# w_out times phi for four row tiles at once in the column groups, whole output rows stored for the last twelve token tiles, and another step list

## The chip, the cores and the metric

One core of one Trainium2 chip runs the kernel. The number that counts is the device time of one execution in microseconds, the median of several runs. The engines are named as in the profile: PE (matrix products; PEld is its weight loading), DVE, ACT and POOL (element-wise work), SP (whose queue issues all DMAs of this kernel).

## The reference

Three stages follow one another. The first is a linear attention with a decaying state, for 4 batches, 8 heads, 768 tokens and head size 48:

```python
for t in range(S):
    cur = einsum('bhd,bhe->bhde', u * k[t], v[t])
    y[t] = einsum('bhd,bhde->bhe', r[t], state + cur)
    state = w[t][..., None] * state + einsum('bhd,bhe->bhde', k[t], v[t])
```

Its output, as 3072 tokens by 384, goes through `h = x @ w_in` (384 to 2048), `g = h * cos(h)` and `x2 = g @ w_out` (2048 to 384). The third stage is a soft mixture: `logits = x2 @ phi` (32 slots), a softmax over the tokens gives the 32 slot inputs, eight experts of two matrices each (`w1`: 384 to 1024, relu, `w2`: 1024 to 384) work on 4 slots each, and a softmax over the slots mixes the slot outputs into 3072 rows of 384. `w_in` and `w_out` come as float64, everything else as float32.

## The kernel before

The kernel never forms `x2`. As only `x2 @ phi` and sums over tokens are needed, it computes `P = w_out @ phi` (2048 by 32) once and takes the logits as `g @ P`; the slot inputs come from sums of `g` over tokens, multiplied by `w_out` at the end.

Work is cut into small named steps, and the string `HEAD` (from line 899) gives their order, about 1980 of them. Each step issues the instructions of one function on one or two engines, and every engine, and SP's queue, works through its own instructions in the order of the list. `name.j` is a step on attention tile j (24 tiles of 128 tokens), `name.g.i` one on token group g (12 groups of 256 tokens) and block i (8 blocks of 256 columns of the hidden layer).

- Weights. `raw` loads a piece of `w_in` ("i") or `w_out` ("o"), and `abs` (ACT), `mx`, `d1`, `d2a`, `d2b` (DVE) turn its float64 bits into float32; the last one of `w_out` is `d2b.o.7`. `whi`, `wn`, `wc` split `w_in` into two halves. `raw` has two buffers.
- `P`. For each of the 16 row tiles m of `w_out`, `oT` (line 416) transposes the tile with three products, `oc` (line 421) copies it to SBUF on ACT, and `om` (line 427) multiplies it with `phi`: three float32 products with a stationary operand of 128 by 128 and 32 moving columns. `ps` (line 430) copies four tiles of `P` to SBUF.
- Attention. `wT`, `kT`, `rT` transpose inputs on PE, `scan`, `sr`, `sp`, `ks`, `L`, `mask`, `bo`, `z`, `st` are DVE's, `A`, `U`, `kN`, `y`, `yb` are PE's, `ru`, `bv`, `zl` POOL's.
- Hidden layer. `h` (lines 451 to 453) is nine products for 128 columns; `turns` (ACT), `rest` (DVE), `cos` (ACT), `mul` (DVE) make `g`; `gT` transposes it (PE), `gc` copies it (ACT), `l` (line 496) adds the block to the logits with four products in the column groups: stationary operands of 32 columns whose outputs lie in the four quarters of the partitions.
- Softmax over tokens: `sum`, `lc`, `max`, `exp`, `xt`, `xr`, `xd`, `dT`, `dc`, `ltok`, `E`, `es`. The last group uses ACT's Exp itself (line 540), the others go by Silu. The step `tab` (line 688) runs one small Exp on ACT.
- `att` closes the attention's buffers and queues the first six expert matrices; `we.6` to `we.10` load others into buffers that the hidden layer has given up.

Behind the list, `hidden(e)` uses `w1[e]`, `expert_out(i, e)` (line 826) uses `w2[e]` for columns 0 to 255 (i = 0) or 256 to 383 (i = 1), with four products at a time in the column groups, and `outputs(i, n0)` (line 843) multiplies the mixing weights with the slot outputs, copies the result to SBUF and stores it. The first four token tiles use the float32 copies `cf` and `so`; the others use `cr` and `sr`, three rounded parts stacked in 96 rows. All of columns 0 to 255 are stored as pairs of token tiles, in runs of 1024 bytes, and then all of columns 256 to 383 as fours, in runs of 512 bytes.

Of the kernel before, what the change touches and what calls it, by code (L numbers as in the profile page):

```python
# [21 lines left out]
def rwkv_moe_kernel(ctx: ExitStack, tc: tile.TileContext, r, k, v, w, u, w_in, w_out, phi, w1, w2, cst, out):  # L22
# [612 lines left out]
    if True:  # L635
# [112 lines left out]
        with tc.manual_schedule(engines=ORDERED):  # L748
# [94 lines left out]
            def outputs(i, n0, tile_=None):  # L843

                cols = parts[i]
                n = cols.stop - cols.start
                nt = 512 // n
                t0, t1 = (0, nt) if tile_ is None else (tile_, tile_ + 1)
                ps = pb(f"o{i}_{n0}_{t0}").rearrange("p (t f) -> p t f", t=nt)[:, 0:t1 - t0]
                if n0 % 6 == 0 and t0 == 0:  # L850
                    obs[i] = wu_p.tile([128, 6, nt, n], F32, tag=f"wu{n0 // 6 if i == 0 else 2}", name=f"ob{i}_{n0}")
                ob = obs[i][:, n0 % 6, t0:t1]
                for t in range(t0, t1):
                    tt = n0 * nt + t
                    if tt < 4:

                        nc.tensor.matmul(ps[:, t - t0], lhsT=cf[:, tt * 128:(tt + 1) * 128], rhs=so[:, cols], start=True, stop=True)
                    else:
                        nc.tensor.matmul(ps[:, t - t0], lhsT=cr[:, tt // NB, tt % NB, :], rhs=sr[:, cols], start=True, stop=True)
                if tile_ is not None and n0:  # L860
                    nc.vector.tensor_copy(ob, ps)
                    if t1 < nt:
                        return
                    ob, t0 = obs[i][:, n0 % 6], 0
                else:
                    (nc.vector.tensor_copy if n0 % 2 else nc.scalar.copy)(ob, ps)
                nc.sync.dma_start(out[(n0 * nt + t0) * 128:(n0 * nt + t1) * 128, cols].rearrange("(t p) f -> p t f", p=128), ob)
# [35 lines left out]
A.0 z.0.1 mask.0 wn.0.0 raw.o.0 st.0.1 lk.2 kT.1 rz.0.1 rz.0.0 lv.1 mx.o.3 d1.o.3 ks.1 d2a.o.3 wn.0.1 wc.0.1 d2b.o.3 lw.2 y.0 lz.2
abs.o.0 lr.2 lw.3 z.1.0 lv.2 A.1 yb.0 mx.o.0 d1.o.0 abs.o.2 mx.o.2 wc.0.0 kN.1 ksn.1 d2a.o.0 d2b.o.0 oT.1 xh.0 xl.0 d1.o.2 raw.i.1
abs.o.1 mx.o.1 d1.o.1 oT.0 oc.0 oc.1 om.0 d2a.o.1 d2a.o.2 wT.2 wf.2 d2b.o.1 om.1 lz.1 raw.i.4 mask.1 d2b.o.2 oT.3 oT.2 oc.2 oc.3
U.1 ru.1 bo.1 oT.4 rz.1.0 abs.i.1 st.1.0 z.1.1 rz.1.1 st.1.1 bv.1 scan.2 kT.2 abs.i.4 om.2 ks.2 y.1 yb.1 om.3 mx.i.4 xh.1 xl.1
mx.i.1 d1.i.1 d2a.i.1 kN.2 d2b.i.1 h.0.2.0 h.0.2.1 ksn.2 oc.4 rT.2 sr.2 sp.2 L.2 raw.i.3 lr.3 lw.4 d1.i.4 z.2.0 d2a.i.4 d2b.i.4
whi.1 wn.1.0 h.0.0.0 wc.1.0 h.0.0.1 turns.0.0 rz.2.0 oT.5 wT.3 oc.5 rest.0.0 ru.2 bo.2 bv.2 U.2 wf.3 A.2 cos.0.0 wn.1.1 st.2.0
turns.0.2 wc.1.1 mul.0.0 gT.0.0 om.4 lk.3 kT.3 mask.2 z.2.1 st.2.1 scan.3 ks.3 rest.0.2 whi.4 abs.i.3 mx.i.3 d1.i.3 sr.3 d2a.i.3
d2b.i.3 sp.3 wn.4.0 kN.3 ksn.3 wn.4.1 h.0.1.0 h.0.1.1 wc.4.0 lw.5 raw.i.6 abs.i.6 lv.4 whi.3 gc.0.0 lk.4 mx.i.6 cos.0.2 wc.4.1  # L910
wn.3.0 oT.7 wc.3.0 rT.3 wn.3.1 raw.i.5 d1.i.6 rz.2.1 oc.7 y.2 wc.3.1 d2a.i.6 turns.0.1 abs.i.5 mul.0.2 L.3 A.3 wT.4 h.0.3.0
d2b.i.6 wf.4 mx.i.5 d1.i.5 z.3.0 whi.6 mask.3 wn.6.1 ps.0 wc.6.1 rest.0.1 scan.4 yb.2 om.5 cos.0.1 xh.2 kT.4 d2a.i.5 ru.3 lk.5
wn.6.0 mul.0.1 sr.4 lv.3 ks.4 l.0.1 xl.2 sp.4 d2b.i.5 U.3 st.3.0 raw.i.7 abs.i.7 z.3.1 mx.i.7 oT.6 wc.6.0 gT.0.2 gc.0.2 lr.5 bo.3
st.3.1 d1.i.7 oc.6 d2a.i.7 h.0.3.1 gT.0.1 wT.5 wf.5 kN.4 h.0.4.0 gc.0.1 d2b.i.7 lz.3 whi.7 wn.7.0 whi.5 h.0.4.1 wn.5.1 lr.4
# [144 lines left out]
```

## Time and profile before

| | |
|---|---|
| median of 3 runs | 563.93 us (563.49 to 565.99) |
| the profiled execution | 567.16 us |
| its span, first to last instruction | 565.4 us |
| PE, PEld, DVE busy | 516.0, 447.6, 438.7 us |
| ACT, POOL busy | 313.3, 123.2 us |
| moved by DMA | 61.75 MB read, 4.72 MB written |

The profiled execution is one run; its time is its span and 1.8 us around it. Busy time of PE contains the latency of its pipeline, so an engine that is 97% busy may still wait a little between products. The span has four parts: the filling up to about 123 us, in which the weights are decoded and the first attention tiles and hidden blocks start; a long stretch up to 520.5 us, where the list of steps ends; the wait for the last expert matrices up to 544.1 us; and the output up to 565.4 us.

### The profile page before, as it was taken

The numbers are of one execution on the slowest core, as the hardware profiler recorded it, in microseconds if no ns is written. First come the engines' busy times: TensorE is split into PE (matmuls) and PEld (weight loads), VectorE is DVE, ScalarE is ACT, GpSimd is POOL, SyncE is SP. The second block draws the span as 40 slices with busy tenths as digits, with TensorE's granted clock in tenths as the row PEclk, the third lists the DMA queues.
The fourth block names the chain that finished last, engine by engine and source line by source line (L and its number), as shares of the span: only waits on it lengthen the run. The fifth ranks groups of instructions, "written<-read, shape, count | busy, mean of one in ns | idle before, by whom it ended". The sixth has DMA issues, their size and how long they took to land.

```text
span 565.4 us, 16220 instructions
## 1 busy us (share of the span) xinstructions
PE 516.0 (91%) x6846; PEld 447.6 (79%) x6846; DVE 438.7 (78%) x823; ACT 313.3 (55%) x657; POOL 123.2 (22%) x163
## 2 busy tenths in 40 slices
...
GB/s 206 297 167 88 144 179 126 128 71 16 112 55 75 68 33 58 44 72 43 45 86 39 61 16 90 41 106 51 59 59 12 6 225 378 180 237 225 405 202 275
DMA packets 146712, 67.52 MB, mean 119 GB/s; under 512 B 127568, under 2 KB 134736, under 8 KB 146640
## 3 DMA queue, kind: packets, MB, share of 16 engines
...
q8 instruction: 54, 0.88, 0.7%
...
HBM read 61.75 MB, written 4.72 MB: 118 GB/s over the span
## 4 chain that ended last, share of the span: by engine, by line
PE 58%; DVE 27%; ACT 6%; DMA 4%; issue 3%; SPq 0%; DVEq 0%; ACTq 0%
PE h L451 9%; PE h L453 8%; PE h L452 8%; PE gT L483 5%; PE l L496 3%; PE y L288 3%; PE E L592 3%; DVE g L475 3%; DMA we<-in_moe_w_dram 3%; PE A L208 3%; DVE L L222 3%; DVE g L467 3%; DVE L L187 2%; PE U L259 2%; DVE qt L156 2%
## 5 line engine op out<-in xcount | busy, mean ns | idle before, releaser
L451 PE MATMUL h<-x,wu 128*128 128x256 f32 x573 | 168.8, 295 | 3.9 <-DVE g L475 3.6
L453 PE MATMUL h<-x,wu 128*128 128x256 f32 x573 | 162.3, 283 | 0.0
L452 PE MATMUL h<-x,wu 128*128 128x256 f32 x573 | 162.3, 283 | 0.0
L451 PEld LDWEIGHTS h<-x,wu 128*128 128x128 f32 x573 | 110.3, 193 | 6.1 <-DVE g L475 5.2
L452 PEld LDWEIGHTS h<-x,wu 128*128 128x128 f32 x573 | 110.4, 193 | 0.2
L453 PEld LDWEIGHTS h<-x,wu 128*128 128x128 f32 x573 | 110.0, 192 | 0.0
L471 ACT ACTIVATE g<-g,half_pi 128x512 f32<-128x512 f32 (+1 forms) x97 | 69.2, 718 | 44.0 <-DVE g L467 43.4
L463 ACT ACTIVATE g<-h 128x512 int32<-128x512 f32 x96 | 56.9, 595 | 59.1 <-PE h L453 39.1
L467 DVE SCALAR_TENSOR_TENSOR g<-g,h 128x512 f32<-128x512 int32 x96 | 64.9, 678 | 27.5 <-ACT g L463 26.8
L475 DVE TENSOR_TENSOR g<-g,h 128x512 f32<-128x512 f32 x96 | 64.7, 678 | 22.9 <-ACT g L471 22.2
L251 POOL TENSOR_TENSOR bv<-vz,bo 64x384 f32<-64x384 f32 x48 | 41.9, 873 | 151.8 <-DVE bo L243 56.6
L488 ACT COPY gt<-gT 128x512 f32<-128x512 f32 x92 | 53.4, 584 | 28.5 <-PE gT L483 22.5
L483 PE MATMUL gT<-cs,g 128*128 128x128 f32 x384 | 58.9, 278 | 2.4 <-DVE g L475 1.7
L169 POOL TENSOR_TENSOR ru<-rn,u_b 128x384 f32<-128x384 f32 x24 | 27.7, 1156 | 123.2 <-DVE bo L243 46.0
L483 PEld LDWEIGHTS gT<-cs,g 128*128 128x128 f32 x384 | 43.6, 142 | 12.3 <-issue 6.5
L274 ACT COPY rzs<-z 64x192 f32<-64x192 f32 x96 | 33.4, 348 | 9.5 <-DVE z L269 8.4
L156 DVE TENSOR_TENSOR_SCAN qt<-wf,one_b 128x520 f32<-128x520 f32 x24 | 31.9, 1329 | 6.5 <-ACT wf L151 6.4
L187 DVE TENSOR_TENSOR L<-rT,pt 64x512 f32<-64x512 f32 x48 | 32.9, 686 | 4.3 <-PE y L288 2.8
L222 DVE TENSOR_TENSOR L<-A,cs 64x512 f32<-64x512 f32 x48 | 33.1, 689 | 1.2
L193 POOL MEMSET L<- 64x512 f32 x32 | 16.6, 520 | 69.3 <-PE y L288 68.3
L496 PE MATMUL l<-g,p_sb 128*32 128x256 f32 x384 | 29.8, 385 | 1.5 <-DVE g L475 1.5
L164 DVE TENSOR_TENSOR_SCAN pt<-wf,ini_f 128x520 f32<-128x520 f32 x24 | 30.2, 1258 | 0.2
...
## 6 DMA issues: line engine op xcount, KB each, us to landing
...
```

The lines of the kernel that those rows point to most:

```text
L187: nc.vector.tensor_tensor(out=L[h, a], in0=ps[h], in1=segs(pt, 0, C)[h], op=ALU.mult)
L222: nc.vector.tensor_tensor(out=L[h, a], in0=ps[h], in1=mask[h].unsqueeze(1).to_broadcast([64, NS, C]), op=ALU.mult)
L451: nc.tensor.matmul(hp, lhsT=wh, rhs=xh[:, c, :], start=(c == 0), stop=False)
L452: nc.tensor.matmul(hp, lhsT=wh, rhs=xl[:, c, :], start=False, stop=False)
L453: nc.tensor.matmul(hp, lhsT=wl, rhs=xh[:, c, :], start=False, stop=(c == KD - 1))
L463: nc.scalar.activation(gt.bitcast(I32), hp, AF.Copy, bias=0.25, scale=1.0 / TWO_PI)
L467: nc.vector.scalar_tensor_tensor(out=gt, in0=gt.bitcast(I32), scalar=-TWO_PI, in1=hp, op0=ALU.mult, op1=ALU.add)
L471: nc.scalar.activation(gt, gt, AF.Sin, bias=half_pi[:, 0:1])
L475: nc.vector.tensor_tensor(out=gt, in0=gt, in1=hp, op=ALU.mult)
L483: nc.tensor.transpose(ps[:, tt, mm, :], gt[:, mm, tt * 128:(tt + 1) * 128], ident)
L488: (nc.vector.tensor_copy if NBK * g + i >= ATT and i in (1, 2) else nc.scalar.copy)(t, pend.pop(("gT", g, i)))
L496: nc.tensor.matmul(lps_t[g][32 * mm:32 * mm + 32, 0:G], lhsT=p_sb[:, m, :], rhs=g_t[g, m // 2][:, m % 2, :], start=(m < 4), stop=(m >= MF ...
```

## The change

It has three parts.

First, `P`. The transposed tiles `wt` take their buffers from the twelve that `gc` uses. `om` now works on four row tiles at once: `phi` is the stationary operand (32 columns), the four transposed tiles are the moving operands of 128 columns, and the outputs lie in the four quarters of the partitions. This leaves the transpose of `P`, so `pc` copies it to SBUF (ACT), `pT` transposes it (one product on PE) and `ps` copies it into `p_sb`. The 16 `om` steps become four, and four `pc` and four `pT` are new.

Second, the output. Columns 0 to 255 of token tiles 0 to 11 are stored as before, in pairs; the last twelve token tiles wait for both halves of the slot outputs and are stored as whole rows, two rows to a partition, 3072 bytes in one run; columns 256 to 383 of the first twelve come last. Only tiles 0 and 1 use `cf`. The slot outputs are copied by ACT and DVE, half each, and the copies of the output alternate between ACT and DVE. `expert_out(1, e)` is spread otherwise between the stores.

Third, `HEAD` has the same steps apart from those of `P`, in another order. A function for `wlo` on another engine is added, and no step uses it.

```diff
     def e_oc(m):
-        wt_t[m] = aw.tile([128, KD, 128], F32, tag="wt", name=f"wt{m}")
+        wt_t[m] = gt_p.tile([128, KD, 128], F32, tag="gt", name=f"wt{m}")
         nc.scalar.copy(wt_t[m], pend.pop(("woT", m)))
-    def e_om(m):
-        if not pt_ps:
-            pt_ps[0] = ps_m.tile([128, MF, SL], F32, tag="m", name="pp")
+    def e_om(u_):
+        ps = ps_m.tile([128, 512], F32, tag="m", name=f"pt{u_}")
         for c in range(KD):
-            nc.tensor.matmul(pt_ps[0][:, m, :], lhsT=wt_t[m][:, c, :], rhs=phi_sb[:, c, :], start=(c == 0), stop=(c == KD - 1))
+            for q in range(4):
+                nc.tensor.matmul(ps[32 * q:32 * q + 32, 0:128], lhsT=phi_sb[:, c, :], rhs=wt_t[4 * u_ + q][:, c, :], start=(c == 0), stop=(c == KD - 1))
+        pt_ps[u_] = ps
+    def e_pc(u_):
+        wt_t["p", u_] = aw.tile([128, 128], F32, tag="pts", name=f"pts{u_}", bufs=1)
+        nc.scalar.copy(wt_t["p", u_], pt_ps[u_][:, 0:128])
+    def e_pT(u_):
+        pend["P", u_] = tps(f"P{u_}")[:, 0:128]
+        nc.tensor.transpose(pend["P", u_], wt_t["p", u_], ident)
     def e_pw(u_):
-        nc.scalar.copy(p_sb[:, 4 * u_:4 * u_ + 4, :], pt_ps[0][:, 4 * u_:4 * u_ + 4, :])
+        nc.scalar.copy(p_sb[:, 4 * u_:4 * u_ + 4, :], pend.pop(("P", u_)).rearrange("p (q s) -> p q s", q=4))
...
+            def store(i, tag, tiles, n):
+                cols = slice(0, DM) if i is None else parts[i]
+                w = cols.stop - cols.start
...
+                        if tt < 2 and i == 0:
+                            nc.tensor.matmul(ps[:, t], lhsT=cf[:, tt * 128:(tt + 1) * 128], rhs=so[:, cols], start=True, stop=True)
+                        elif i is None:
+                            o = tiles[0] * 128 + b0 + t
+                            nc.tensor.matmul(ps[:, t], lhsT=crt[:, o:o + 255:2], rhs=sr[:, cols], start=True, stop=True)
...
+                    pend["ob"] = 1 - pend.get("ob", 0)
+                    (nc.scalar.copy if pend["ob"] else nc.vector.tensor_copy)(ob[:, b0:b0 + k], ps)
+                dst = out[t0:t0 + len(tiles) * 128, cols]
+                nc.sync.dma_start(dst.rearrange("(p t) f -> p t f" if i is None else "(t p) f -> p t f", p=128), ob)
...
-            nc.scalar.copy(so[:, parts[0]], ops[0][:, 0:256])
-            expert_out(1, 0)
-            outputs(0, 0, 0)
+            copy_so(0)
+            store(0, "wu0", [0], 0)
             slots_out(0)
+            store(0, "wu0", [1], 1)
             slots_round(0)
-            outputs(0, 0, 1)
-            outputs(0, 1, 0)
-            outputs(0, 1, 1)
-            for n0 in range(2, 5):
-                outputs(0, n0)
-            for e in range(1, 4):
+            for e in range(2):
                 expert_out(1, e)
-            for n0 in range(5, 9):
-                outputs(0, n0)
-            for e in range(4, NE):
+            for t in range(2, 8, 2):
+                store(0, "wu0", [t, t + 1], t)
+            for e in range(2, 5):
                 expert_out(1, e)
-            nc.vector.tensor_copy(so[:, parts[1]], ops[1][:, 0:128])
-            for n0 in range(9, 12):
-                outputs(0, n0)
+            for t in range(8, 12, 2):
+                store(0, "wu0", [t, t + 1], t)
+            for e in range(5, NE):
+                expert_out(1, e)
+            copy_so(1)
             slots_out(1)
             slots_round(1)
-            for n0 in range(6):
-                outputs(1, n0)
+            for t in range(12, 18, 2):
+                store(None, "wu1", [t, t + 1], t - 12)
+            for t in range(18, 24, 2):
+                store(None, "wu2", [t, t + 1], t - 18)
+            for t in range(0, 12, 4):
+                store(1, "wu3", [t, t + 1, t + 2, t + 3], t)
```

Of the list, three places are spoken of below. Where the weights' decoding ends:

```diff
-h.1.1.0 h.1.1.1 mask.5 tab turns.0.6 gc.0.5 rest.0.6 gT.0.4 kT.6 cos.0.6 oc.10 sr.6 sp.6 mul.0.6 ks.6 oT.13 oc.13 rz.5.0 om.10
-gc.0.4 ps.2 wf.7 rT.6 mx.o.7 d1.o.7 h.1.0.0 oT.12 oc.12 d2a.o.7 d2b.o.7 close l.0.5 om.13 oT.14 oT.15 om.12 turns.1.1 bv.4 ru.6
+oc.11 wT.6 lw.8 U.5 om.2 gc.0.4 rest.0.7 cos.0.7 wf.6 L.5 A.5 mx.o.7 d1.o.7 bo.4 bv.4 mul.0.6 oT.13 oc.13 mask.5 d2a.o.7 d2b.o.7
+close h.1.0.0 gT.0.6 oT.12 pc.2 pT.2 oc.12 lr.6 gc.0.6 scan.6 h.1.0.1 ru.6 mul.0.7 sr.6 ps.2 bo.6 oT.14 oT.15 oc.14 l.0.5 oc.15
+om.3 kT.6 turns.1.0 rest.1.0 rz.4.0 h.1.1.0 gT.0.7 ks.6 pc.3 pT.3 ps.3 z.5.0 st.5.0 z.5.1 st.5.1 cos.1.0 mul.1.0 y.4 l.0.7 rT.6
```

The new place of `tab` (before, it stood as shown above):

```diff
+turns.9.2 rT.23 dT.8 h.9.4.0 xl.22 cmb.1.5 zl.23 rest.9.2 sp.23 cos.9.2 gT.9.1 L.23 gc.9.1 h.9.4.1 gT.8.6 h.9.5.0 h.9.5.1 gc.8.6
+xh.21 xl.21 dc.8 tab turns.9.4 cmb.0.5 rest.9.4 turns.9.5 h.9.6.0 gT.9.3 h.9.6.1 rest.9.5 cos.9.5 mul.9.2 A.23 ltok.8 E.8.0 E.8.1
```

And the end, where the last hidden block was `h.11.7` in two halves and is now the undivided `h.11.4`:

```diff
-rest.11.4 gT.11.2 dT.10 ltok.10 gc.11.0 mul.11.5 cos.11.4 mul.11.4 h.11.7.0 dc.10 turns.11.7.0 h.11.7.1 turns.11.7.1 rest.11.7.0
-cos.11.7.0 rest.11.7.1 mul.11.7.0 l.11.5 cos.11.7.1 E.10.0 mul.11.7.1 l.11.7 gT.11.4 gc.11.2 gc.11.4 gT.11.5 sum.11 lc.11 max.11
+rest.11.5 cos.11.5 gT.11.2 gc.11.2 xd.10 h.11.4.0 h.11.4.1 turns.11.4 dT.10 mul.11.5 ltok.10 gT.11.6 dc.10 E.10.0 E.10.1 gc.11.3
+rest.11.4 cos.11.4 mul.11.4 l.11.5 mul.11.7.0 l.11.7 sum.11 we.6 we.10 gT.11.5 lc.11 gc.11.5 gT.11.4 gc.11.6 max.11 quart.11
```

## Rows read from the trace of the kernel before

**Rows 1.** The page: busy time of each engine.
```profile
PE 516.0 (91%) x6846; PEld 447.6 (79%) x6846; DVE 438.7 (78%) x823; ACT 313.3 (55%) x657; POOL 123.2 (22%) x163
```

**Rows 2.** Four stages: PE, PEld, DVE, ACT, POOL busy (count), clock, DMA share, GB/s.
```profile
20.00:123.00 103.00, 84.91 (x967) 70.95 (x965) 92.89 (x141) 56.81 (x109) 26.22 (x24) 0.90 0.63 148
123.00:520.50 397.50, 386.68 (x5263) 345.85 (x5263) 317.24 (x625) 236.18 (x506) 83.69 (x103) 1.00 0.37 88
520.50:544.10 23.60, 23.00 (x390) 13.83 (x390) 8.86 (x25) 8.05 (x21) 5.86 (x9) 1.00 0.88 335
544.10:565.40 21.30, 13.61 (x204) 11.65 (x204) 7.19 (x13) 6.13 (x13) 0.00 (x0) 0.90 0.73 224
```

**Rows 3.** DVE in order of time (start, duration): the last step of the decoding.
```profile
121.47 0.90 DVE L374 SCALAR_TENSOR_TENSOR wo_sb<-rawo,ao 128x768 int32<-128x768 int32 x1
```

**Rows 4.** Groups by line: w_out times phi (busy, mean ns, idle before).
```profile
L427 PE MATMUL pp<-phi_sb,wt 128*128 128x32 f32 x96 | 13.2, 280 | 0.6 <-ACT wt L421 0.6
```

**Rows 5.** PE in order of time (start, duration): `l`, `om`, two `oT`, `om`, `h`.
```profile
130.75 0.64 PE L496 MATMUL l<-g,p_sb 128*32 128x256 f32 x8
131.32 0.85 PE L427 MATMUL pp<-phi_sb,wt 128*128 128x32 f32 x6
132.01 0.85 PE L416 MATMUL woT<-cs,wo_sb 128*128 128x128 f32 x6
132.70 0.75 PE L427 MATMUL pp<-phi_sb,wt 128*128 128x32 f32 x6
133.29 0.36 PE L451 MATMUL h<-x,wu 128*128 128x256 f32 x1
```

**Rows 6.** The chain that ended last: start, time on it, what.
```profile
463.82 0.86 PE l L496 x16
469.91 0.87 PE gT L483 x8
...
500.27 0.12 PE h L452
...
528.61 15.46 DMA we<-in_moe_w_dram
...
546.80 1.29 PE o L857 x6
...
551.41 1.88 PE so L826 x64
```

**Rows 7.** PE in order of time: one `gT` step, then two `l` steps.
```profile
448.53 0.60 PE L483 MATMUL gT<-cs,g 128*128 128x128 f32 x4
449.06 1.07 PE L496 MATMUL l<-g,p_sb 128*32 128x256 f32 x16
```

**Rows 8.** DVE work of an attention tile: two pieces of the chain, one group by line.
```profile
347.32 0.69 DVE ks L199
409.60 1.15 DVE qt L156
...
L269 DVE TENSOR_TENSOR z<-st_state,qt 128x192 f32<-128x192 f32 x44 | 21.0, 478 | 0.8
```

**Rows 9.** `turns` for half a block (order of time) and for a whole one (group).
```profile
510.25 0.38 ACT L463 ACTIVATE g<-h_7b 128x256 int32<-128x256 f32 x1
...
L463 ACT ACTIVATE g<-h 128x512 int32<-128x512 f32 x96 | 56.9, 595 | 59.1 <-PE h L453 39.1 <-PE l L496 16.7 <-PE gT L483 2.9
```

**Rows 10.** DMA: 550-553 us (1024-byte stores), 559-562 (512-byte), 524-539 (loads), 562-566 in fortieths.
```profile
DMA packets 1058, 1.02 MB, mean 340 GB/s; under 512 B 63, under 2 KB 1058, under 8 KB 1058
...
DMA packets 1734, 0.86 MB, mean 288 GB/s; under 512 B 54, under 2 KB 1734, under 8 KB 1734
...
DMA packets 2022, 6.06 MB, mean 404 GB/s; under 512 B 62, under 2 KB 62, under 8 KB 2019
...
DMA  9999999999999999996100000000000000000000
```

**Rows 11.** ACT in order of time: one of its table loads.
```profile
123.41 1.28 ACT L471 ACT_TABLE_LOAD   x1
```

More of the change, by code (lines that the diff above doesn't have):

```diff
@@ L841, in rwkv_moe_kernel @@
             obs = {}
[L843 to L867, printed above, removed]
@@ L869, in rwkv_moe_kernel, with copy_so @@
+            def copy_so(i):
+                c, h = parts[i], (parts[i].start + parts[i].stop) // 2
+                nc.scalar.copy(so[:, c.start:h], ops[i][:, 0:h - c.start])
+                nc.vector.tensor_copy(so[:, h:c.stop], ops[i][:, h - c.start:c.stop - c.start])
             expert_out(0, 0)
@@ L903 @@
[L903 to L914, printed above, removed]
@@ L915 @@
-raw.o.5 bv.3 turns.0.3 rest.0.3 rz.3.0 scan.5 ksn.4 wn.5.0 turns.0.4 rest.0.4 wc.7.0 raw.o.4 lz.4 abs.o.4 mx.o.4 wc.5.0 wc.5.1
-rz.3.1 ru.5 bo.5 rT.4 L.4 cos.0.4 om.7 ru.4 wn.7.1 lr.6 om.6 cos.0.3 d1.o.4 d2a.o.4 mul.0.3 ps.1 wc.7.1 abs.o.5 U.4 z.4.0 rz.4.0
-st.4.0 z.4.1 st.4.1 rz.4.1 d2b.o.4 y.3 mul.0.4 l.0.3 A.4 yb.3 xh.3 kT.5 ks.5 mask.4 h.0.5.0 xl.3 h.0.5.1 lw.6 lk.6 raw.o.6 rT.5
-mx.o.5 lz.5 d1.o.5 turns.0.5 kN.5 ksn.5 sr.5 rest.0.5 oT.8 gT.0.3 oc.8 oT.9 sp.5 d2a.o.5 gc.0.3 bo.4 oc.9 d2b.o.5 cos.0.5 h.0.7.0
@@ L919 @@
-h.0.7.1 lv.5 bv.5 turns.0.7 wT.6 om.9 wf.6 mul.0.5 gT.0.5 rest.0.7 L.5 oT.11 raw.o.7 U.5 A.5 oc.11 om.11 z.5.0 scan.6 st.5.0
-abs.o.6 mx.o.6 z.5.1 lw.7 abs.o.7 d1.o.6 d2a.o.6 st.5.1 rz.5.1 om.8 cos.0.7 z.6.0 d2b.o.6 mul.0.7 h.0.6.0 h.0.6.1 wT.7 oT.10
-h.1.1.0 h.1.1.1 mask.5 tab turns.0.6 gc.0.5 rest.0.6 gT.0.4 kT.6 cos.0.6 oc.10 sr.6 sp.6 mul.0.6 ks.6 oT.13 oc.13 rz.5.0 om.10
-gc.0.4 ps.2 wf.7 rT.6 mx.o.7 d1.o.7 h.1.0.0 oT.12 oc.12 d2a.o.7 d2b.o.7 close l.0.5 om.13 oT.14 oT.15 om.12 turns.1.1 bv.4 ru.6
@@ new lines @@
+d2b.i.4 cos.0.2 d1.i.3 turns.0.0 z.2.1 A.2 d2a.i.3 st.2.1 whi.4 wn.4.0 wc.4.0 wn.4.1 wc.4.1 rest.0.0 mul.0.2 mask.2 raw.i.6
+abs.i.6 sr.3 d2b.i.3 wT.4 kT.3 ks.3 h.0.1.0 pT.0 cos.0.0 h.0.1.1 lz.3 mx.i.6 ru.2 bo.2 lk.4 bv.2 ps.0 sp.3 raw.i.5 whi.3 wn.3.0
+lr.4 wc.3.0 wn.3.1 mul.0.0 wc.3.1 gT.0.2 oT.6 turns.0.1 rT.3 abs.i.5 d1.i.6 d2a.i.6 gc.0.2 h.0.3.0 rest.0.1 h.0.3.1 L.3 cos.0.1
+wf.4 oc.6 mul.0.1 rz.2.1 d2b.i.6 whi.6 raw.i.7 lw.6 gT.0.0 A.3 scan.4 sr.4 gc.0.0 wn.6.0 mask.3 mx.i.5 sp.4 d1.i.5 l.0.1 wn.6.1
@@ new lines @@
+wc.6.1 d2a.i.5 turns.0.3 kN.3 rest.0.3 abs.i.7 ksn.3 mx.i.7 h.0.4.0 wc.6.0 kT.4 ks.4 lv.3 gT.0.1 d2b.i.5 z.3.0 cos.0.3 U.3 st.3.0
+oT.7 gc.0.1 lv.4 oc.7 raw.o.4 wT.5 wf.5 whi.5 om.1 ru.3 lk.5 y.2 rz.3.0 yb.2 xh.2 d1.i.7 d2a.i.7 z.3.1 st.3.1 wn.5.1 d2b.i.7
+wn.5.0 whi.7 pc.1 abs.o.4 h.0.4.1 scan.5 xl.2 wc.5.1 wn.7.0 turns.0.4 mul.0.3 mx.o.4 d1.o.4 d2a.o.4 d2b.o.4 rest.0.4 z.4.0 wc.5.0
+wc.7.0 raw.o.5 rz.3.1 abs.o.5 mx.o.5 h.0.5.0 h.0.5.1 wn.7.1 wc.7.1 pT.1 ps.1 bo.3 bv.3 turns.0.5 rest.0.5 rT.4 kN.4 ksn.4 cos.0.5
@@ new lines @@
+bo.9 lk.11 ks.10 E.1.0 E.1.1 bv.9 y.8 lr.11 cos.2.7 mul.2.7 gc.2.5 l.2.5 l.2.7 rT.10 lr.12 h.3.1.0 h.3.1.1 yb.8 zl.10 rz.9.1
+mask.9 es.1 sum.2 turns.3.1 sp.10 L.10 gT.2.6 gc.2.6 lz.10 lv.10 lc.2 h.3.0.0 h.3.0.1 A.10 wT.11 rest.3.1 cos.3.1 mul.3.1 mask.10
+gT.2.4 xh.8 xl.8 rz.9.0 wf.11 turns.3.0 gc.2.4 h.3.2.0 rest.3.0 cos.3.0 mul.3.0 h.3.2.1 gT.3.1 gc.3.1 kT.11 kN.10 turns.3.2
+scan.11 ks.11 h.3.3.0 h.3.3.1 y.9 lv.11 ksn.10 l.3.1 U.10 max.2 exp.2 rest.3.2 xt.2 cos.3.2 xr.2 mul.3.2 z.10.0 gT.3.0 xd.2 dT.2
@@ new lines @@
+wT.13 wf.13 mul.4.2 st.12.1 scan.13 sr.13 h.4.3.1 gT.3.7 h.4.5.0 h.4.5.1 wT.14 turns.4.3 rest.4.3 exp.3 xt.3 z.13.0 cos.4.3
+mul.4.3 l.4.1 l.4.3 rz.11.1 y.11 xr.3 gc.3.7 yb.11 lz.13 lw.15 xd.3 dT.3 ltok.3 gT.4.0 turns.4.5 gc.4.0 rest.4.5 cos.4.5 h.4.4.0
+h.4.4.1 ks.13 dc.3 E.3.0 E.3.1 mul.4.5 sp.13 wf.14 scan.14 sr.14 turns.4.4 xh.11 rest.4.4 cos.4.4 mul.4.4 rT.13 gT.4.2 kN.13
+gc.4.2 ksn.13 h.4.7.0 h.4.7.1 xl.11 es.3 gT.4.3 gc.4.3 bv.13 h.4.6.0 turns.4.7 rest.4.7 zl.13 rz.13.0 gT.4.4 L.13 h.4.6.1 U.13
```

193 lines of the change are left out of this document (102 added, 91 removed).

## The prediction

> **What bounds the kernel now.** I read the page first, then the span cut into its stages, then the chain that ended last with PE and DVE in order of time beside it, then the DMA totals of the tail. PE is busy 516.0 of 565.4 us, DVE 438.7, ACT 313.3 [rows 1]. Cut by stages it is another picture [rows 2]. From 20 to 123 us DVE is busy 92.89 of 103 us, a share of 0.90, and PE 84.91; PE's clock averages 0.90, so it spends part of this at the lower of its two levels (1.2 and 2.4 GHz). The stage ends with the decoding of the weights: the last such step begins at 121.47 [rows 3]. From 123 to 520.5 us PE is the bound, busy 386.68 of 397.5 us at full clock, DVE 317.24. From 520.5 to 544.1 us the last expert matrices stream in (335 GB/s over the stage, 404 GB/s in its middle [rows 10]); the chain shows it as one wait of 15.46 us from 528.61 [rows 6]. After that come 21.3 us of output, in which DMA is busy 0.73 of the time and PE 13.61 us [rows 2].
>
> So the list ends when PE has done its work, what it has left at 123 us decides that, and the filling before it goes at DVE's pace. The tail of 23.6 + 21.3 us hangs on DMA.
>
> **P = w_out times phi.** Before, one `om` takes 0.69 us (131.32 to 132.01) and another 0.59 (132.70 to 133.29) [rows 5]; the 96 records of the group are 16 such steps of 6 [rows 4]. At 0.64 that is 10.2 us of PE. The new `om` has the form of `expert_out(1, e)`: stationary 32 columns, moving 128, outputs in the four quarters. The trace has 64 records of it in 1.88 us [rows 6], 0.0294 each; a new `om` has 24 (twelve products, two records each), so 0.70 us. If the quarters did not run side by side, nothing would be left of the gain.
>
> It also changes the shape in which the array is used, twice per `om`. Two `gT` steps take 0.87 us, 0.44 each, but one that is followed by `l` takes 0.53 (448.53 to 449.06) [rows 6, 7]: 0.09 for going into the column groups. Two `l` take 0.86, 0.43 each, one followed by `om` 0.57 (130.75 to 131.32) [rows 5, 6]: 0.14 for coming out. I add 0.24 per `om`, and 0.11 for `pT`, an eighth of the 0.87. Four times 1.05 is 4.2 us, so PE saves 6.0. A rule that speaks against the change: the Trainium skill, "TensorEngine Tiling (Array Packing)", section Key Properties, says that changing the tiling mode drains TensorE. The trace agrees that it costs something, by 0.09 and 0.14 us here; without it the saving would be 7.0.
>
> `pc` is a wait added to PE: `pT` waits for ACT, and everything behind it on PE waits too. No row shows `pc`; it reads 128 columns, so it costs less than `turns` with 512 (0.595 us [rows 9]) and more than nothing. Between `om.u` and `pT.u` the new list has 11, 9, 5 and 3 other PE steps, with three, three, one and one `h` among them (nine products at 0.12 [rows 6], 1.08 us each), so I cost the wait at nothing for the first three. The last has 1.08 us and two steps of 0.44 to cover it, with `turns.1.0` and `rz.4.0` ahead of `pc.3` on ACT, and may cost up to 1 us; I take nothing. `oc` now takes buffers from `gc`'s twelve. Counting live tiles along the list I never come above twelve; nothing, as long as a buffer need not come free in order.
>
> **What the filling gives back.** By PE alone the 6.0 us would all come off. But the filling runs at DVE's pace and PE has gaps there, so I do it once more by DVE. Up to `d2b.o.7` the new list has one attention tile less begun: `scan`, `sp` (1.15 each), `ks` (0.69), a `mul` as long as `ks`, and seven short ones, `z` at 0.48 being the kind shown [rows 8]; for these I take 2.5 us, an estimate, so 6.2 us in all. At a busy share of 0.90 decoding ends 6.9 us sooner. PE then has more left: three transposes of four at 0.44, three `h` at 1.08 and one `oT` (half of 0.69), 4.9 us, plus one new `om`, its switches and two `pT` (1.2), less four old `om` (2.6): 3.5 us more, 3.6 at the stage's 397.5 : 386.68. That leaves 3.3 us. Neither engine alone is the bound of the filling, so I take the middle of 3.3 and 6.0, 4.6 us, and keep both ends. The list also begins with another order of loads: a whole piece of 768 KB before half a piece, and the small attention loads between. 384 KB more ahead of the first decoding is 1.0 us at 404 GB/s [rows 10], in either direction; I take nothing, since the same bytes are wanted by the time the decoding ends.
>
> **The long stretch.** All else in the list has the same steps, and PE's waits there come to 10.8 us (397.5 less 386.68). The new order can save or add some of it. I take nothing and keep a third of it, 3.6 us, both ways. Moving `tab` takes ACT's table loads (one for the Exp, one of 1.28 us at 123.41 for the next `cos` [rows 11], and one at the next Silu) out of the filling and into this stretch. What waits there on ACT is `turns` and `cos` behind two loads, 2.6 + 0.6 us. Behind the new place PE has both `h.9.6` (2.2 us), `gT.9.3` (0.4), two `E` of eight column-group products (twice an `l`, 0.86 each) and `A.23`, which need none of it: over 4.3 us. So it is hidden; uncovered, the three loads are worth 3.8 us.
>
> **The end of the list.** The last hidden block was halved and is now whole. `turns` on half takes 0.38 us, on a whole 0.595 [rows 9]; with `rest`, `cos` and `mul` differing alike, the chain behind the last `h` is 0.9 us longer, and what PE has to fill it (`E.10`, `gT.11.6`) has run out before. So -0.9. The three late matrices wait for `E.11.1` as before, and the 23.6 us behind it stay.
>
> **The output.** Before, stores run at 340 GB/s with runs of 1024 bytes and at 288 with 512 [rows 10], and the last compute step is not what ends the kernel. Now PE reaches the second half of `so` sooner: two `cf` products fewer (1.29 us for three, 0.43 each [rows 6]) and four other tiles fewer, 1.2 us off 553.3 (551.41 + 1.88 [rows 6]); with copy, rounding and the first pair of rows, whole-row stores begin at about 554.3, an estimate. By then DMA has had only 1.57 MB to store and idles some of the time. Left are 2.36 MB in runs of 3072 bytes and 0.79 MB in runs of 512. From 288 and 340 GB/s, one engine of 16 needs 28 and 48 ns a run, 20 more for 512 bytes more, hence 127 ns for 3072: 386 GB/s, near the 404 of the loads. So 6.1 + 2.7 us, and with 0.3 to start, 563.4, against 564.0, when the stores end now (DMA is idle from the 21st fortieth of 562 to 566 [rows 10]): 0.6 saved. If long runs went no faster than 288, it would be 10.9 us, 1.5 lost; at 404, 0.8 saved. The Trainium skill, "DMA: Bandwidth & Descriptors", section Specifications, puts the smallest transfer for line rate at 512 bytes, by which long runs would gain nothing; the two store rates here differ by 18% above that size, so I give that little weight.
>
> **Sum.** 4.6 - 0.9 + 0.6 = 4.3 us off the profiled execution's 567.16, 562.9. That execution lies 3.2 us above the median of the three runs, 563.93; the same 4.3 off the median gives 559.6.
>
> **Rivals.** (B) The saved PE time falls wholly into gaps that PE has in the filling anyway. For it: DVE's 0.90 there. Against it: the list starts less DVE work ahead of the decoding. Time: 563.9 + 0.9 - 0.6 = 564.2. (C) PE bounds all of it, and a third of the waits goes too: 6.0 - 0.9 + 0.6 + 3.6 = 9.3 off, 554.6. (D) Slower: on top of B the table loads at `tab`'s new place stall PE. Price 3.8 us, 568.0; it decides from the point where ACT lags by more than about 1 us there, since two loads and `turns` (3.2 us) must fit under the 4.3 us of queued PE work. ACT is busy 236 of 397.5 us in the stretch [rows 2], which speaks against it. (E) The column groups do not run side by side: the time of B, 564.2. (F) Long runs store no faster than short ones: 559.6 + 2.1 = 561.7.
>
> **How the numbers follow.** Forecast 0.50, B 0.17, C 0.17, D 0.11, E 0.03, F 0.02. A difference under 0.5% (2.8 us, so 561.1 to 566.7) is about what a measurement of this kernel cannot tell from no change. Of the forecast I put 0.44 below 561.1 and 0.06 above. Faster: 0.44 + 0.17 = 0.61; same: 0.06 + 0.17 + 0.03 + 0.02 - 0.02 = 0.26, with 0.02 of B reaching beyond; slower 0.13. The range reaches from C's 554.6 less the unknowns of the start and the tail (1.0 + 0.2) and some of the waits, 552.5, to 566.5, which is B with the tail's other end (564.2 + 2.1, rounded up); D is left out.
>
> **What would show it.** In the new profile the group of `om` should have 96 records again but about 3 us of PE steps in all; the last decoding step should begin at about 115 us; the gap from the list's end to the last matrix should stay near 23.6 us and the last part be 20.5 to 21 us with stores above 360 GB/s while whole rows go out. The prediction is wrong if the decoding ends no sooner than 121 us, if PE's waits in the long stretch grow by more than 4 us, or if the stores fall behind 300 GB/s.

## The result, and the profile after

The kernel after takes 551.58 us (median, 549.88 to 552.63), beside 564.96 us for the kernel before in the same comparison: a ratio of 0.975, 95% interval 0.972 to 0.979, 13.4 us off. The forecast of 559.6 us had the direction and a third of the size, and the lower end of its range lay 0.9 us above the measured time. The profiled execution of after took 552.63 us, its span is 550.8, against 567.16 and 565.4 before.

Busy time of the engines in the profile page of after, to be held against [rows 1]: PE is busy for 8.7 us less.

```profile
PE 507.3 (92%) x6832; PEld 437.9 (80%) x6832; DVE 433.2 (79%) x825; ACT 315.8 (57%) x663; POOL 124.8 (23%) x163
```

Where the decoding of the weights ends is told by the group of its last operation (duration minimum, median, maximum in ns, then the first and the last start). First before, then after:

```profile
L374 DVE SCALAR_TENSOR_TENSOR wo_sb<-rawo,ao x8: 895/950/959, 29.4 to 130.7; 128x768 int32<-128x768 int32 x8
...
L374 DVE SCALAR_TENSOR_TENSOR wo_sb<-rawo,ao x8: 932/954/1692, 30.0 to 115.9; 128x768 int32<-128x768 int32 x8
```

The first of these rows shows a misreading in the prediction: the step at 121.47 [rows 3] is the seventh of eight, the last one begins at 130.7. So the filling lasted to 131.6 us before, and not to about 123. In after the last step itself is a long one, 1.67 us:

```profile
114.78 1.95 POOL L169 TENSOR_TENSOR ru<-rn,u_b 128x384 f32<-128x384 f32 x1
...
115.88 1.67 DVE L374 SCALAR_TENSOR_TENSOR wo_sb<-rawo,ao 128x768 int32<-128x768 int32 x1
```

The decoding ends at 117.5 there, 14.1 us sooner.

The span cut at that point and at the end of the list. First before (two stages), then after (four), columns as in [rows 2]:

```profile
20.00:131.60 111.60, 93.50 (x1029) 78.88 (x1027) 100.37 (x152) 62.55 (x120) 26.22 (x24) 0.89 0.59 136
131.60:520.50 388.90, 378.09 (x5204) 337.93 (x5203) 309.76 (x615) 230.45 (x495) 83.69 (x103) 1.00 0.38 90
...
20.00:117.54 97.54, 81.19 (x1002) 65.65 (x1000) 90.99 (x144) 57.54 (x112) 21.16 (x19) 0.91 0.70 164
117.54:504.50 386.96, 380.06 (x5230) 340.43 (x5230) 313.60 (x626) 237.72 (x505) 89.01 (x108) 0.99 0.38 90
504.50:529.00 24.50, 24.33 (x410) 14.93 (x406) 8.93 (x25) 7.93 (x21) 5.87 (x9) 0.97 0.83 321
529.00:550.80 21.80, 13.07 (x170) 11.23 (x170) 7.32 (x15) 6.37 (x15) 0.00 (x0) 0.75 0.64 218
```

| | before | after | change | forecast |
|---|---|---|---|---|
| decoding ends | 131.6 | 117.5 | -14.1 | -6.9 |
| from there to the end of the list | 388.9 | 387.0 | -1.9 | +4.5 |
| end of the list to the last expert product of columns 0 to 255 | 24.7 | 24.5 | -0.2 | 0 |
| from there to the end | 20.2 | 21.8 | +1.6 | -0.6 |
| sum | | | -14.6 | -3.0, with the middle of two views -4.3 |

Cut like this, nearly all of the gain lies in the filling. But the small change behind it is a sum of larger ones, as the next table shows: PE waits 6.2 us less in the long stretch, and has some 1 us more work left and loses some 3 us more at the end of the list. To see what happens inside the list I put every PE record to its step, gave each step the time it takes undisturbed (`h` 1.08, `gT` 0.42, `E` 0.86 us and so on) and call "waits" what is left between a step's begin and the sum of the steps ahead of it. The sum of all steps is 442.6 us before and 435.6 after. Waits contain all that keeps PE from its pace, the lower clock too. `h.1.7` is a block soon after the filling, `h.11.0` the first of the last token group, `E.11.1` the last product of the list.

| kernel (profiled execution) | `h.1.7` begins | PE work ahead of it | waits from there to `h.11.0` | waits from `h.11.0` to `E.11.1` | `E.11.1` begins |
|---|---|---|---|---|---|
| before | 159.2 | 105.9 | 20.1 | 4.1 | 519.2 |
| new om alone (c1) | 159.7 | 98.9 | 18.6 | 4.0 | 518.2 |
| new list, old om (c2) | 148.8 | 105.5 | 13.9 | 6.4 | 505.3 |
| new filling, old rest (c5) | 152.5 | 98.9 | 18.4 | 4.1 | 510.8 |
| old filling, new rest (c6) | 162.7 | 98.5 | 13.0 | 6.2 | 518.1 |
| after | 146.1 | 98.5 | 13.9 | 6.4 | 502.6 |

### The profile page after: what moved, and what is told of

Same layout as the page of the kernel before. It is cut to its first block, busy times and chain, and to the rows that moved or that the text cites. A ratio compares the mean times of both kernels' runs of the same rounds, so it can differ in the third digit from the quotient of the medians.

```text
span 550.8 us, 16214 instructions
## 1 busy us (share of the span) xinstructions
PE 507.3 (92%) x6832; PEld 437.9 (80%) x6832; DVE 433.2 (79%) x825; ACT 315.8 (57%) x663; POOL 124.8 (23%) x163
## 4 chain that ended last, share of the span: by engine, by line
PE 64%; DVE 16%; ACT 8%; DMA 5%; SPq 4%; issue 2%; ACTq 0%; DVEq 0%
PE h L462 9%; PE h L464 9%; PE h L463 9%; PE gT L494 6%; PE E L603 4%; PE l L507 3%; PE y L288 3%; PE A L208 3%; PE U L259 2%; PE so L838 2%; DMA rawi<-in_moe_w_in_dram 2%; PE hps L797 2%; DVE g L478 2%; DVE L L222 2%; ACT g L482 2%
## 5 line engine op out<-in xcount | busy, mean ns | idle before, releaser
L462 PEld LDWEIGHTS h<-x,wu 128*128 128x128 f32 x573 | 108.9, 190 | 3.5 <-DVE g L486 1.7
L463 PEld LDWEIGHTS h<-x,wu 128*128 128x128 f32 x573 | 109.1, 190 | 0.2
L464 PEld LDWEIGHTS h<-x,wu 128*128 128x128 f32 x573 | 108.7, 190 | 0.0
L251 POOL TENSOR_TENSOR bv<-vz,bo 64x384 f32<-64x384 f32 x48 | 43.8, 912 | 140.5 <-DVE bo L243 54.4
L164 DVE TENSOR_TENSOR_SCAN pt<-wf,ini_f 128x520 f32<-128x520 f32 x24 | 31.7, 1321 | 0.1
L288 PEld LDWEIGHTS y<-L,rzs 128*32 128x32 f32 x1536 | 25.0, 112 | 6.6 <-ACT rzs L274 2.3
```

The costliest lines, as they stand in the source:

```text
L251: nc.gpsimd.tensor_tensor(out=bv[h], in0=vn_t[j][h, :, c, :], in1=bo[h].to_broadcast([64, H, D]), op=ALU.mult)
L288: nc.tensor.matmul(ps[m:m + 32, o, c * C:(c + 1) * C], lhsT=rz[:, c, p, a, 32 * b:32 * b + 32], rhs=L[:, a, 2 * p + c, :], start=m not in ...
L462: nc.tensor.matmul(hp, lhsT=wh, rhs=xh[:, c, :], start=(c == 0), stop=False)
L463: nc.tensor.matmul(hp, lhsT=wh, rhs=xl[:, c, :], start=False, stop=False)
L464: nc.tensor.matmul(hp, lhsT=wl, rhs=xh[:, c, :], start=False, stop=(c == KD - 1))
```

## Experiments

All ratios are to the kernel before on the same chip, with 95% intervals; 0.001 is 0.57 us.

### The parts one by one

`c1` is the old list and output with the new `om`; `c2` the new list and output with the old `om`; `c3` the old kernel with the new output; `c4` and, on another chip, `e4` the new kernel with the old output; `e3` the new list alone; `c9` the kernel after once more. Wherever the new list or the new `om` stands, the transposed tiles have `gc`'s buffers; no run tries that move by itself. In the lists of `c1` and `c2`:

```diff
 c1:
-om.0 ... om.1 ... om.2 ... ks.2 y.1 yb.1 om.3
+ks.2 y.1 yb.1 om.0 pc.0
...
-ps.0
+pT.0 ps.0
 c2, e3:
-om.0
+om.0 om.1 om.2 om.3
-pc.0
-pT.0
```

> The kernel before, its list and its output, with only the new form of om: om.u stands where the fourth old om of its quartet stood, pc.u right behind it, pT.u ahead of ps.u. Two theories. (PE) PE's work is what decides the end of the list, from the filling on: the comparison of the two traces counts 442.6 us of PE steps in the old list and 435.6 in the new one, so the new form alone takes 7.0 us off, 564.96 - 7.0 = 558.0. (Filling) The filling goes at DVE's pace and the saved time falls into PE's gaps there, rival B of the prediction: 564.5 to 565.5, no change. Half of it, the middle that the prediction took, would be 561.5.

> The kernel after, with its list and output, but P by the 16 old products: four old om stand where each new om stood, pc and pT are gone, the transposed tiles keep the buffers of gc. (PE) The 7.0 us of PE work come back in full: 551.58 + 7.0 = 558.6, and the order of the list alone would then be worth 6 us or more. (Filling) The new order ends the decoding by DVE's pace whatever PE does: 551.6 to 553, and the order would be worth nearly all of the gain.

> The kernel before with only the new output part. By the prediction's term (whole-row stores begin 9.1 us behind the last column-0-to-255 product of the experts) 0.6 us are saved: 564.4. By the trace of after, where the whole-row stores begin 11.6 us behind that product and the stage from there to the end is 21.8 us against 20.2, the new output is 1.6 us slower: 566.6.

> The kernel after with the output part of the kernel before. If the new output loses 1.6 us, this is faster than the kernel after: 551.58 - 1.6 = 550.0. If it saves the 0.6 us of the prediction, 552.2. If the output's length follows from the state in which the list leaves the tail (TensorE's granted clock was 0.82 in the last 31 us of after and 0.90 in the last 21 of before), nothing changes: 551.6.

> The kernel after once more, beside the three others on one chip, as the value that they are compared with: 0.975 of before, as it was. The profile tells what of the filling's times changes from execution to execution: the decoding ended at 116.9 us in one and at 115.3 in the kernel with the old output part, whose list is the same.

> The new list with the old om (four in the place of each new one, no pc and pT, buffers of gc) and the old output: what the order alone is worth. With the new output it was 0.9841 of before. If the output costs 1.6 us as the traces say, 0.981, about 555; if 4.7 us as the times of after with the old output say, 0.976, about 552.5. With om alone at 1.0049, the order would then be the whole of the gain and the new om worth its 5 us only inside it.

> The kernel after with the old output once more, on the same chip as the three others, since its time (0.9671 of before) and its trace (tail 1.5 us shorter from the first rounding of the slot outputs on) don't agree on the output's share: 0.972 if the trace is right, 0.967 if the time is.

| | ratio | interval |
|---|---|---|
| c1, om alone | 1.0049 | 1.0028 to 1.0071 |
| c3, output alone | 1.0032 | 1.0010 to 1.0054 |
| e3, list alone | 0.9824 | 0.9779 to 0.9870 |
| c2, list and output | 0.9841 | 0.9794 to 0.9888 |
| c4, list and om | 0.9671 | 0.9646 to 0.9696 |
| e4, the same | 0.9702 | 0.9671 to 0.9734 |
| c9, all three | 0.9756 | 0.9735 to 0.9778 |

The order alone is worth 10 us. The profiles agree: the last decoding step begins at 130.7 us before, 127.7 in `c1`, 116.9 in `c2` and 115.9 in after. (The ends of 116.9 and 115.3 in the expectation of `c9` take the usual duration; with the last step's own, 1.67 and 1.66 us, they are 117.5 and 115.9.) The new `om` is worth nothing in the old order and 5 to 7 us in the new one (c2 against c9, on two chips: 0.0085, interval about 0.003 to 0.014; e3 against e4, on one chip: 0.0122, about 0.007 to 0.018), so the two parts belong together. Some of this price comes from executions at a lower clock: five of the twelve of `c2` and `e3` took 558 us and more, at a mean granted clock of 0.960 to 0.967; the other seven took 552.4 to 555.2 at 0.972 to 0.979, 2 to 5 us more than the same kernels with the new `om`. The output costs 1.8 us in the old kernel; in the new one the old output is 3 to 5 us better, which is a version faster than both kernels: 547.78 and 548.50 us.

That `om` alone is slower by 2.8 us, and not equal, I can't settle. Its profiled execution, the fastest of its twelve, ends the list 1.0 us sooner. PE's waits behind its decoding show one thing that `om` brought in: `pT.3` begins 2.3 us late, at 136.89. It does not wait for `pc.3`, which ends at 132.42, but for DVE, which ends `L.6`, the step ahead of `y.4` and `pT.3` in the list, at 136.43. In the kernel after, no `pT` waits.

```profile
PE P L438 <- DVE ini_f L160: 2.3, 1, 2.3
```

### Which half of the list

`c5` has the new list up to `ps.3` (`P` complete) and all remaining steps in the old order; `c6` is the counterpart. `c8` puts `tab` back behind `close`.

> The kernel after with its list up to ps.3, where P is complete, and from there on all remaining steps in the order of the old list; new om, new output. (Filling decides) What the filling leaves behind decides the rest: the decoding ends at about 117 us, and the old order behind it keeps most of that, 552 to 555. (Stretch decides) By the count of PE's waits in the two traces the filling gave 5.7 us and the stretch behind it 6.1; then the 6.1 are lost and the end of the list gives 2.3 back: 555.5. If the order of the stretch is what matters most, over 560.

> The counterpart: the old list with the new om up to ps.3, then all remaining steps in the order of the new list; new output. (Filling decides) The decoding ends at 128.6 us as in the run with om alone, and the new order behind it can't make up for it: 562 to 566. (Stretch decides) 6.1 us come back from the stretch: about 558. If the order of the stretch is what matters most, 553 to 556.

> The kernel after with tab where it stood before, behind the end of the decoding. The prediction has its table loads hidden at both places: 551.6 on the median. If they cost in the filling what they take, two loads of 1.28 us and the small Exp lie on the way of PE: up to 3.8 us more, 555.4. If the new place of tab costs (rival D), this is faster, down to 547.8.

`c5`: 0.9942 (0.9922 to 0.9962), 561.83 us. `c6`: 1.0054 (1.0037 to 1.0071), 567.99 us. `c8`: 0.9768 (0.9745 to 0.9791), 552.05 us, beside 0.9756 for `c9`.

`c5` by itself would speak for the order of the stretch, `c6` for the filling: both lose most of the gain, so neither half is enough, and `c6` lies above all that was expected of it. The table of waits tells why: the waits from `h.1.7` to `h.11.0` follow the order that stands there (18.4 and 18.6 with the old, 13.0 and 13.9 with the new), whatever filling came before. And each seam costs: `c6` lies at `h.1.7` 3.0 us behind `c1`, `c5` 6.4 us behind after, likely since the steps that one order had put off are not where the other expects them; no run shows the reason. `tab` costs nothing measurable at either place (0.7 us, give or take 1.8).

### Whose pace the filling goes at

`d1` and `d3` add DVE work to the filling of after and before, `d2` and `d4` PE work.

```diff
 d1, d3 (ten pieces of weights):
-mx.i.4
+mx.i.4 mx.i.4
 d2, d4:
-        for c in range(KD):
+        twice = (g, i, mm) in ((0, 0, 1), (0, 1, 1), (0, 3, 1), (0, 4, 1), (0, 5, 1))
+        for c in list(range(KD)) * (2 if twice else 1):
```

> The kernel after with 5.6 us more work on DVE in the filling and none elsewhere: the step mx (0.56 us, a maximum in place, so that twice is the same as once) is done twice on ten of the pieces of weights. (DVE's pace) If the filling goes at DVE's pace, all of it comes out at the end: 551.5 + 5.6 = 557.1. (PE's pace) If PE bounds the filling, DVE's waits take it: 551.5 to 552.5. (Chain) If the two hang on each other step by step, between them, some 554.

> The kernel after with 5.4 us more work on PE in the filling and none elsewhere: five of the h halves of token group 0 do their nine products twice, 1.08 us each, the second time from zero again. (DVE's pace) PE's gaps take it: 551.5 to 552.5. (PE's pace) 551.5 + 5.4 = 556.9. (Chain) some 554. In the new list the old om, 7.0 us of PE work more, cost 5.2 us, interval 2 to 8, which speaks for more than half.

> The kernel before with the same 5.6 us more of DVE work in the filling. (DVE's pace) 564.9 + 5.6 = 570.5. (PE's pace) 565 to 566. Before, DVE stood idle for 11 of the 111.6 us from 20 to the end of the decoding, so the price should be a little lower here than in the kernel after, if DVE's pace decides there.

> The kernel before with the same 5.4 us more of PE work in the filling. The run with om alone took 7.0 us of PE work from this filling and won nothing. If that is because PE has gaps there (DVE's pace), adding is as cheap as taking away: 565 to 566. If it is because the old order had been fitted to the old om and any edit costs, adding costs more than its own length: 570.3 or above.

The ratios of `d1` and `d2` are to be held against that of `c9`, measured on another chip:

| | ratio | interval | beside | `E.11.1` begins later, than in `c9` (d1, d2) or before, by |
|---|---|---|---|---|
| d1, after + 5.6 us of DVE | 0.9794 | 0.9755 to 0.9833 | 0.9756 | 5.6 us |
| d2, after + 5.4 us of PE | 0.9771 | 0.9733 to 0.9809 | 0.9756 | 1.5 us |
| d3, before + 5.6 us of DVE | 1.0090 | 1.0060 to 1.0119 | 1 | 5.5 us |
| d4, before + 5.4 us of PE | 1.0013 | 0.9985 to 1.0040 | 1 | -0.2 us |

In the kernel before the times are clear: DVE's work comes out at the end with 5.1 of 5.6 us, PE's with 0.7 of 5.4 (interval -0.8 to 2.3), its profile with none. In the kernel after the times give 2.1 us for DVE's and 0.8 for PE's, each within 2.5 us or so; its profiles give 5.6 and 1.5. The profiled execution of `d1` was its slowest, at a mean granted clock of 0.963 where the other five had 0.976 to 0.984, so the 5.6 us are not all DVE's; the price in the kernel after likely lies between the two. Last decoding steps of `d1` and `d3`:

```profile
L374 DVE SCALAR_TENSOR_TENSOR wo_sb<-rawo,ao x8: 930/950/1693, 30.1 to 120.1; 128x768 int32<-128x768 int32 x8
...
L374 DVE SCALAR_TENSOR_TENSOR wo_sb<-rawo,ao x8: 895/948/959, 28.1 to 135.2; 128x768 int32<-128x768 int32 x8
```

They begin 4.2 and 4.5 us later than in after and before, with 5.6 us of DVE work added. In the kernel before, DVE is the engine whose work ahead of the decoding counts. For the kernel after this is likely, but its times alone do not tell DVE's price from PE's.

### The end of the list

PE's waits there, first before, then after (in all, times, longest), and the last `E` steps in the chain that ended last, of before, after and `f1`:

```profile
PE dT L568 <- ACT dl L540: 1.6, 1, 1.6
...
PE dT L579 <- ACT dl L551: 2.5, 1, 2.5
PE E L603 <- ACT dt L586: 1.0, 2, 0.8
```

```profile
518.34 2.18 PE E L592 x30
...
500.89 3.64 PE E L603 x32
...
499.41 2.18 PE E L603 x30
```

The clock in the stretches around that wait, before, after, `f1`:

```profile
516.00:520.00 4.00, 2.43 (x35) 1.57 (x37) 1.27 (x6) 3.09 (x8) 0.00 (x0) 1.00 0.07 25
...
498.00:502.00 4.00, 2.44 (x17) 1.53 (x21) 1.33 (x4) 2.95 (x8) 0.82 (x1) 0.62 0.59 228
502.00:506.00 4.00, 3.97 (x30) 1.93 (x22) 1.91 (x7) 0.34 (x1) 0.00 (x0) 0.53 0.48 125
...
498.00:502.00 4.00, 3.23 (x39) 1.88 (x39) 1.46 (x5) 2.17 (x8) 0.82 (x1) 1.00 0.17 25
```

After waiting 2.48 us for the Exp of the last group, PE goes on at the lower level of its clock, and `E.11` takes 3.64 instead of 2.18 us. `e1` and `e2` move two steps, `f1` and `f2` give the end its old order (the list up to `turns.10.6` as in after); `e2` and `f2` have the old output too.

```diff
 e1, e2:
-dc.10 E.10.0 E.10.1 gc.11.3
+dc.10 gc.11.3
-lc.11 gc.11.5
+lc.11 E.10.0 E.10.1 gc.11.5
```

> The kernel after with two steps of the list's end moved: E.10.0 and E.10.1 stand behind lc.11 instead of ahead of l.11.5. In the trace of after PE waits 0.82 us for them at 491.9 (before: none), then 2.48 us for the Exp of the last group (before: 1.56), the granted clock falls to 0.50 from 499 to 505 (before it stays at 1.00 there) and E.11 takes 3.64 us instead of 2.16. (Cover) If PE's work stood at the wrong place, the two E fill the wait, the chain through the Exp begins some 2 us sooner and the clock does not fall: 2.5 to 4 us less than 551.5, so 547.5 to 549. (Tail) If the expert matrices are what ends the tail, as in the kernel before, the list ends sooner and the tail is longer by the same: 551 to 552.

> The same with the output part of the kernel before. If the end of the list and the output are two separate losses of the change, they add: 2.5 to 4 us under the kernel after with the old output (547.8), so 544 to 545.5. If not, 547 to 548.

> The kernel after, new output, with its list up to turns.10.6, and all that is left (the end of group 10, group 11 with its last block in two halves, the last expert matrices) in the order of the old list. (End) If the new end of the list costs the 2.2 us of waits and the some 1.5 us of fallen clock that the traces show behind h.11.0, this is 3 to 4 us faster than after: 547.5 to 548.5, ratio to before 0.969. (Tail) If the last matrices or the stores take it up again, 551 to 552, ratio 0.975.

> The same with the output part of the kernel before too, so that of the change there remain the new om and the order up to group 10. After with the old output measured 0.967 and 0.970 of before, 548.2 on the median. (End) 3 to 4 us less, 544 to 545.5, ratio 0.963, the fastest of all. (Tail) 548, ratio 0.969.

`e1`: 0.9765 (0.9730 to 0.9801). `e2`: 0.9750 (0.9718 to 0.9781). `f1`: 0.9687 (0.9661 to 0.9713), 548.14 us. `f2`: 0.9692 (0.9669 to 0.9714), 548.00 us.

`e1` was the wrong cure. PE's waits at the end of its list:

```profile
PE l L507 <- DVE g L486: 2.8, 1, 2.8
PE dT L579 <- ACT dl L551: 2.2, 1, 2.2
```

The two `E` had covered the wait for the last undivided block; moved, they leave it open, and the wait for the Exp hardly shrinks. The old order with the block in two halves is 3.8 us better than after by the times (0.0069, interval about 0.0035 to 0.010), and its clock stays at 1.00. In the profiles `E.11.1` begins 1.4 us sooner than in `c9`, and `E.11` then takes 1.5 us less.

With the old end, the old output brings nothing more (`f2`), although in every pair of profiles the tail behind the slot outputs' first product is 1.4 to 1.6 us shorter with it. By the times the old output gains 1.8 (c3), 3 to 5 (c4, e4), 0.9 (e2) and -0.3 us (f2); I take the 1.5 us of the traces as the likeliest and leave the rest open.

### The output in the trace

The DMA's share in fortieths, from the last expert product of columns 0 to 255 to the end: before (545 to 565.4), then after (529 to 550.8).

```profile
DMA  1000061719999999999499999999999999999000
...
DMA  0000164301999977086007999999999999999400
```

The rate while whole rows go out (543 to 545 us) and while 512-byte runs do (547 to 549):

```profile
DMA packets 291, 0.80 MB, mean 398 GB/s; under 512 B 32, under 2 KB 32, under 8 KB 291
...
DMA packets 1168, 0.58 MB, mean 291 GB/s; under 512 B 32, under 2 KB 1168, under 8 KB 1168
```

Long runs are as fast as the forecast wanted (398 for 386 GB/s), and 2.36 and 0.79 MB take 8.8 us as it said. But after has a hole in the middle, where the stores of the first half have run out and the whole rows are not ready. On the Trainium skill's figure, "DMA: Bandwidth & Descriptors", section Specifications, that 512 bytes suffice for line rate, the trace disagrees: 291 GB/s at 512 bytes, 398 at 3072.

## Why the forecast was too small

**P.** Right. The new `om` takes 0.79, 1.05, 0.80 and 1.01 us to the next step; with `pT` some 4.1 us for the 4.2 of the forecast. By the steps the saving is 7.0 us, 1.0 above the forecast, as an old `om` counts 0.69 there and not 0.64. Group and one place in PE's order of time:

```profile
L429 PE MATMUL pt<-wt,phi_sb 128*32 128x128 f32 x96 | 4.0, 297 | 0.0
...
118.92 1.08 PE L429 MATMUL pt<-wt,phi_sb 128*32 128x128 f32 x24
119.93 0.66 PE L141 MATMUL kT<-cs,kn 128*128 128x128 f32 x4
```

The quarters run side by side, so rival E falls, and `pc` costs nothing in the new list, where three steps lie between `om.3` and `pT.3`.

**The filling, the step that failed.** It failed in the term "6.2 us at a share of 0.90, so decoding ends 6.9 us sooner", and twice. The end of the decoding before was read off the seventh step instead of the eighth, 9.2 us too early; this left DVE's share at 0.90 (100.37 of 111.6 us) and so the 6.9 us as they were. And the size was too small, 6.9 us for the 14.1 measured: from 20 us to the decoding's end DVE does 100.37 us of work before and 90.99 after, 9.4 less where 6.2 were counted from the list, and it stands idle for 11.2 us before and 6.6 after, 4.7 less where 0.7 were taken. The forecast had no term for DVE's waits beyond its share of 0.90, and the counting by the list missed that steps do not all cost their usual time there: 11 `z` took 6.2 us before, 9 of them 3.3 after. All steps of DVE that took clearly longer than usual ran beside element-wise work of POOL, such as this `z` (usually 0.35 us):

```profile
117.99 1.22 POOL L170 TENSOR_TENSOR ru<-ru,kn 128x384 f32<-128x384 f32 x1
118.25 1.17 DVE L269 TENSOR_TENSOR z<-st_state,qt 128x192 f32<-128x192 f32 x1
```

Against the median of each form, DVE's steps beside POOL took 6.7 us too long before and 2.8 after, all others none. These 3.9 us and the 6.2 counted make 10.1, near the 9.4. Many other steps beside POOL kept their time, and no run moves POOL's work, so this stays a reading of the traces. Which steps of the new order shorten DVE's waits stays open too. That the last step was then forecast "at about 115 us" and begins at 115.9 is luck, an accident of the two errors.

**What PE has left.** By the steps, 362.7 us at the decoding's end before and 364.0 at 116.9 us after, shortly ahead of it: about 1 more, forecast 3.5. The count by the list was not at fault. When the decoding ended, PE in after had already passed five steps that the list has behind `d2b.o.7` (`h.1.0.0`, `gT.0.6`, `oT.12`, `pT.2`, `h.1.0.1`, some 3 us), and before it had passed only `l.0.5`.

**The middle of two views.** Wrong as a way of reckoning. d3 and d4 show that the old filling counts nearly all of DVE's added work (5.1 of 5.6 us) and little or none of PE's (0.7 of 5.4), and c1 that taking PE's away gives nothing. So rival B was right of the change that it was made for, the new `om` by itself, and the gain came from the other part, the order, which the forecast had put down as moving little. In the new order the saved 7.0 us of `om` are worth 5 to 7, in part by the executions at a lower clock, yet d2's 5.4 us of added `h` cost only 0.8, give or take 2.5. So where PE's work stands seems to matter; no run separates this. Rival C came nearest in time (554.6), for half of its reasons: not PE bounds the filling, but the stretch does give back waits, and more than the third that C took.

**The long stretch.** The second term that failed: taken as 0 with 3.6 us either way; the waits from `h.1.7` to `h.11.0` fell by 6.2 us. The bound was a third of the window less the busy time, 10.8 us, but a busy PE may still be behind its pace: counted by steps the waits were 20.1 us. c5 and c6 show the 5 to 6 us to belong to the order of that stretch; which steps of it they hang on is not shown. The waits that show as idle, before and after, without the last group:

```profile
PE h L451 <- DVE g L475: 2.4, 2, 1.5
PE lc L509 <- ACT lg L503: 1.1, 1, 1.1
PE A L208 <- DVE L L187: 1.0, 3, 0.4
...
PE kN L215 <- DVE ini_f L160: 1.3, 1, 1.3
PE h L462 <- DVE g L486: 0.5, 2, 0.3
```

**tab.** Right within what the times can tell (c8), and rival D's 3.8 us fall.

**The end of the list.** Right in sign, 0.9 us forecast. The waits up to `E.11.1` grew by 2.3 us, of which the fallen clock in `E.11.0` is some 0.8, and `E.11.1` loses as much again; by the times of f1 the whole end is worth 3.8. The cause named, nothing left to fill the chain of the undivided block, is the one that e1 laid open; that the clock would follow was not thought of.

**The output.** Wrong in sign, 0.6 us saved forecast, 1.6 lost in the trace. The rate was right; the start of the whole rows was not. They were to begin 9.1 us behind the last expert product of columns 0 to 255 (554.3 against 545.2) and begin 11.6 us behind it (540.6 against 529.0): PE reaches the second half later by 0.9 us than worked out, and the way from the last product to the first packet, through copy, product, rounding, the first rows and their copy, takes 3.8 us where 2.2 were set down. Rival F falls, as long runs do store faster.

**The start.** Right within what was kept: `y.0` begins at 28.6 us before, 29.4 after.
